# Holding back the first tile's value loads until the keys of the second and third head pair have landed

## The chip, the cores and the metric

The kernel runs on one core of a Trainium2 chip. A core has five engines that run their own instruction streams side by side: TensorE (PE in the profile, with its weight loads as PEld), VectorE (DVE), ScalarE (ACT), GpSimd (POOL) and SyncE (SP). Each engine works strictly through its own list, and waits at an instruction until what it needs is there. Transfers between DRAM and the on-chip memory SBUF are issued by SP, ACT or POOL and carried out by 16 DMA engines that all three share. The metric is the device time of one execution in microseconds (us); of several executions the median is given.

## What is computed

Two stages run one after the other. The first is attention in blocks of 64 tokens, for 8 batches, 8 heads, 576 tokens and a head size of 64:

```
q_c, k_c, v_c = (x.reshape(B, H, 9, 64, 64) for x in (q, k, v))
scores = 1/sqrt(64) * q_c @ k_c.T
attn   = exp(scores - max(scores)); attn = attn / (sum(attn) + 1e-9)
x      = (attn @ v_c) as tokens x (heads * 64)          # 4608 x 512
```

The second is a feed-forward layer on these 4608 rows, with weights 512 x 2048 and 2048 x 512:

```
h   = x @ w_in
g   = h where h >= 1;  0 where h <= -1;  (h + 1)^2 / 4 between
out = g @ w_out
```

All inputs are 4-byte floats, except that each weight comes as 8-byte words, two 32-bit halves of a number, from which the kernel first builds a high and a low part.

## The kernel before

**Tiles.** The 4608 tokens are cut into nine tiles of 512. In each tile the eight heads are taken as four pairs, called g = 0 to 3 here ("head groups" in the change's words). For each pair one tile of q, one of k and one of v is loaded, 128 x 512 floats (256 KB) each. The first tile (t = 0) has places of its own for most of these: the loads for pairs 2 and 3 go into memory in which the last weights will lie later, and are named after that place: `first_wi` in the trace is q and k of pairs 2 and 3, `first_wo` is v of these pairs and also some of the intermediate tiles of this stage. `q_sb`, `k_sb` and `v_sb` hold pairs 0 and 1.

**First tile's attention.** For one pair: TensorE turns q and k around (`flip`, L402), ACT copies the results out (L417), TensorE forms the scores (L435), DVE takes the maximum and subtracts it (L491, L507), ACT forms the exponentials (L510), DVE sums them and takes reciprocals (L516 to L518), POOL multiplies (L523), TensorE turns the result around and ACT copies it (L402, L537), TensorE multiplies by v (L457), and ACT and DVE split the result into a high and a low part (L562, L563). Only L457 needs v.

**Weights.** Each of the 32 weight blocks (wi0 to wi15, wo0 to wo15, 512 KB each) is loaded (L268, L275) and then prepared by three ACT and four DVE instructions (L290 to L319). The feed-forward products (L578 into the hidden layer, L612 out of it) of the first tile follow the weights as they become ready. From the second tile on they stay in SBUF, and attention of later tiles is woven between the products.

**Who sets the order.** Nothing is issued at once. Each step is handed to a `Plan` with the engine it runs on, a cost, what it reads and writes as names, and for loads a `lag` and a time for which the queue is `moving`. `Plan.emit` then plays these costs through and writes out each engine's instructions in the order of its due times. Of two steps that are both due when an engine comes free, the one added earlier goes first. Where TensorE would be idle by the plan, small filler products are put in (L1115, L1118). On the chip, the plan's times play no part any more: only the order within each engine is left, and the true dependences between tiles, on which instructions wait.

**First loads.** The list `first_loads` (L958) says which loads of the first tile go to which queue. q, k and the weights go to SP (k of pair 0 to ACT). The four v tiles go to POOL, in four transfers of 64 KB each (L377), with nothing that they wait for, so they are at the head of POOL's list. The q and k tiles go in two transfers of 128 KB each (L337). After them SP issues the loads of the second tile (L351, L367) and further weights.

Of the kernel before, what the change touches and what calls it, by code (L numbers as in the profile page):

```python
# [9 lines left out]
F32 = mybir.dt.float32  # L10
# [122 lines left out]
def kernel(  # L133
# [15 lines left out]
    nc = tc.nc  # L149
# [4 lines left out]
    P = 128  # L154
    C = 64
# [16 lines left out]
    def turn(t, g):  # L172
        if t <= ALONE:
            return t * NP + g
        d, m = divmod(t - ALONE - 1, 2)
        return (ALONE + 1) * NP + d * 2 * NP + 2 * g + m
# [3 lines left out]
    sb = ctx.enter_context(tc.tile_pool(name="sb", bufs=1))  # L180
    psum = ctx.enter_context(tc.tile_pool(name="psum", bufs=1, space=bass.MemoryType.PSUM))

    def buffers(pool, name, n, dtype=F32):
        return [
            (f"{name}{i}", pool.tile([P, T], dtype, name=f"{name}{i}")) for i in range(n)
        ]
# [3 lines left out]
    q_bufs, k_bufs, v_bufs = (buffers(sb, f"{n}_sb", 2) for n in "qkv")  # L190
# [50 lines left out]
    def room(name, bufs, t, g):  # L241
        if t == 0 and (name, g) in first:
            return first[name, g]
        if t > 0 and name in ("e", "x"):
            return wheel[(2 * turn(t, g) + (name == "x")) % 3]
        return bufs[turn(t, g) % len(bufs)]

    plan = Plan()
# [13 lines left out]
    def load_weight(w, j, queue="sp"):  # L262
        eng = queues[queue]

        def emit():
            words[w, j] = dst = place("words", w, j, [P, 2 * T], U32)
            if w == "wi":
                eng.dma_start(  # L268
                    out=dst.rearrange("p (kc f) -> p kc f", kc=KC),
                    in_=w_in[:, 2 * j * P:2 * (j + 1) * P].rearrange(  # L270
                        "(kc p) f -> p kc f", p=P
                    ),
                )
            else:
                eng.dma_start(out=dst, in_=w_out[j * P:(j + 1) * P, :])  # L275

        plan.add(queue, 0.65, emit, gate["ready"], (f"{w}{j}_0", f"{w}{j}_1"), lag=1.7, moving=1.4)
# [101 lines left out]
                    in_=rows.rearrange(split, r=2)[r],  # L379
                )  # L380

    def load_heads(t, g, which="qkv", queue="sp"):
        eng = queues[queue]

        for n, src, bufs in (("q", q, q_bufs), ("k", k, k_bufs), ("v", v, v_bufs)):
            if n not in which:
                continue
            key, dst = room(n, bufs, t, g)
            load = load_values if n == "v" else load_rows if t == 0 else load_blocks
            rows, parts = (1.4, 2) if load == load_rows else (1.4, 2 if t > 0 and BATCH[t] is not None else 4) if load == load_values else (  # L390
                (2.2, 4) if BATCH[t] is not None else (2.2, 8)
            )
            plan.add(
                queue, 0.65 * parts,
                lambda load=load, dst=dst, src=src: load(eng, dst, src, t, g),
                (), (key,), lag=1.7, moving=rows if queue == "sp" else 1.5 * rows,
            )

    def flip(ps, src):
# [553 lines left out]
    def load_next(n=1):  # L953
# [3 lines left out]

    first_loads = [  # L958
# [4 lines left out]
    ]  # L963
    for which, n, queue in first_loads:
        if which in ("wi", "wo"):
            load_weight(which, n, queue)
            loads.remove((which, n))
        else:
            load_heads(0, n, which, queue)

    for g in range(NP):
        attn_turn(0, g)
# [2 lines left out]
    for g in range(NP):  # L975
        attn_products(values_of(0, g))
        attn_split(0, g)

    load_heads(1, 0, "qk")
    load_next(2)  # L980
    load_heads(1, 0, "v")
    load_next(2)
    load_heads(1, 1)
# [66 lines left out]
    for t in range(ALONE + 1):  # L1050
        for j in range(NF):
# [4 lines left out]
            elif step in SPREAD:  # L1056
                n, m = SPREAD[step]
# [31 lines left out]
    for t in range(ALONE + 1, NTILE, 2):  # L1089
        units = [unit for p in range(NQ) for unit in whole(t, p)]  # L1090
        n = turn(t, 0) + 2 * NP
# [74 lines left out]
```

## Time and profile before

| | |
|---|---|
| time, median of 3 runs | 844.25 us (843.58 to 845.26) |
| the profiled execution | 845.72 us, of which the span on the page is 844.0 us |
| PE busy | 828.6 us (98% of the span) |
| DVE, ACT, POOL busy | 533.9, 469.1 and 272.0 us |
| DMA | 147.89 MB, mean 175 GB/s |
| packets by POOL's queue (q0) and by SP's (q1) | 30720 and 198368 |

The profile is of one execution. A page begins with busy times; the share of an engine over the whole span says little of one stage, so the start of the kernel is read here in views of short windows, in the timeline (each instruction with its start and length and, in brackets, the idle time before it and what ended it), and in the view of one tile's loads (how long an issue took, and how long it then was until the data had landed).

### The profile page before, as it was taken

How to read it: one execution, taken by the hardware profiler on the slowest of the kernel's cores; microseconds unless marked ns; L12 is line 12 of the kernel's file. 1: busy time of each engine (PE TensorE's matmuls, PEld its weight loads, DVE VectorE, ACT ScalarE, POOL GpSimd, SP SyncE). 2: the span in 40 equal slices, each digit the busy share in tenths (PEclk: the TensorE clock that was granted, in tenths of full speed). 3: DMA queues.
4: the chain of work that ended last, by engine and by line, in shares of the span. 5: the costliest groups of instructions: out<-in, count | busy, mean ns of one | idle time of the engine just before them, and what ended most of it. 6: DMA issues, size and time to landing. Idle time of an engine off the chain costs nothing.

```text
span 844.0 us, 16178 instructions
## 1 busy us (share of the span) xinstructions
PE 828.6 (98%) x5774; PEld 678.6 (80%) x5774; DVE 533.9 (63%) x941; ACT 469.1 (56%) x1001; POOL 272.0 (32%) x490
## 2 busy tenths in 40 slices
PE   6998999999999999999999999999999999999997
PEld 6786778888888888888888888888888888888886
DVE  3999997768788666756779427765593234343422
ACT  3889895555666645555566226555572255455422
POOL 5111110454434232343444114343432133333220
PEclk9999999999999999999999999999999999999999
DMA  9888732776878555977788418765545254444432
GB/s 218 231 254 232 227 65 58 205 220 177 217 173 240 102 135 142 260 214 212 205 209 245 157 58 243 215 192 183 173 155 183 62 189 171 153 147 164 152 98 75
DMA packets 230223, 147.89 MB, mean 175 GB/s; under 512 B 188672, under 2 KB 200448, under 8 KB 230144
## 3 DMA queue, kind: packets, MB, share of 16 engines
q0 software_dynamic: 30720, 89.68, 31.8%
q1 hardware_dynamic: 198368, 56.92, 29.2%
q8 instruction: 46, 0.75, 0.4%
q10 hardware_dynamic: 1056, 0.26, 0.2%
q14 instruction: 33, 0.27, 0.1%
HBM read 101.71 MB, written 36.70 MB: 164 GB/s over the span
## 4 chain that ended last, share of the span: by engine, by line
PE 92%; SPq 2%; DVE 2%; ACT 1%; DMA 1%; issue 1%; ACTq 0%; DVEq 0%
PE ps_o L612 45%; PE ps_h L828 27%; PE ps_h L578 15%; PE ps_a L457 2%; PE ps_a L435 2%; SPq L337 2%; DMA words_wi<-in_moe_w_in_dram 1%; PE ps_o L1115 0%; DVE tmp L626 0%; SPq L275 0%; ACT x L500 0%; ACT e L500 0%; SPq L268 0%; DVE tmp L305 0%; DVE tmp L300 0%
## 5 line engine op out<-in xcount | busy, mean ns | idle before, releaser
L612 PE MATMUL ps_o<-parts_wo,gh 128*128 128x512 f32 x1152 | 358.2, 392 | 0.4 <-DVE parts_wo L319 0.2
L612 PEld LDWEIGHTS ps_o<-parts_wo,gh 128*128 128x128 f32 x1152 | 214.6, 188 | 47.2 <-DVE tmp L626 1.5
L612 PE MATMUL ps_o<-parts_wo,gl 128*128 128x512 f32 x576 | 224.6, 390 | 0.0
L828 PE MATMUL ps_h<-x,ring 128*128 128x512 f32 x864 | 219.0, 389 | 0.0
L828 PEld LDWEIGHTS ps_h<-x,ring 128*128 128x128 f32 x864 | 162.2, 188 | 33.9
L599 DVE TENSOR_TENSOR gl<-r,gh 128x512 fp32r<-128x512 f32 x144 | 98.8, 687 | 105.9 <-ACT gh L597 105.0
L597 ACT CAST gh<-r 128x512 fp32r<-128x512 f32 x144 | 89.2, 621 | 129.1 <-PE ps_o L612 94.0
L808 POOL DMA_DIRECT2D ring<-combos x168 | 92.1, 549 | 168.1 <-PE ps_h L828 156.3
L578 PE MATMUL ps_h<-xh,parts_wi 128*128 128x512 f32 x384 | 131.3, 400 | 0.0
L612 PEld LDWEIGHTS ps_o<-parts_wo,gl 128*128 128x128 f32 x576 | 108.2, 188 | 22.9 <-DVE gl L599 0.2
L849 DVE TENSOR_TENSOR h<-ps_h,snaps 128x512 f32<-128x512 f32 x72 | 49.0, 680 | 76.6 <-ACT snaps L680 74.3
L578 PEld LDWEIGHTS ps_h<-xh,parts_wi 128*128 128x128 f32 x384 | 73.1, 190 | 16.3
L532 POOL DMA_DIRECT2D aT<-e x96 | 47.9, 505 | 118.7 <-issue 34.5
L859 DVE SCALAR_TENSOR_TENSOR r<-h,r 128x512 f32<-128x512 f32 x72 | 49.3, 685 | 58.0 <-ACT r L858 57.8
L680 ACT COPY snaps<-ps_h 128x512 f32<-128x512 f32 x72 | 42.1, 585 | 72.9 <-PE ps_h L828 72.2
L855 ACT ACTIVATE r<-h 128x512 f32<-128x512 f32 x72 | 45.5, 632 | 65.2 <-DVE h L849 63.7
L858 ACT ACTIVATE r<-r 128x512 f32<-128x512 f32 x96 | 60.5, 630 | 2.4
L933 POOL DMA_DIRECT2D r<-rest x48 | 26.2, 547 | 100.0 <-DVE gl L599 88.5
L578 PE MATMUL ps_h<-x_parts,parts_wi 128*128 128x512 f32 x128 | 50.7, 396 | 0.0
L897 POOL DMA_DIRECT2D rest<-r x48 | 26.2, 545 | 63.1 <-DVE r L859 62.1
L532 POOL DMA_DIRECT2D aT<-x x48 | 24.1, 506 | 65.1 <-DVE r L589 45.6
L585 ACT ACTIVATE r<-ps_h 128x512 f32<-128x512 f32 x48 | 29.2, 607 | 27.3 <-PE ps_h L578 27.1
(122 smaller groups left out, 969.1 us busy)
## 6 DMA issues: line engine op xcount, KB each, us to landing
ring<-combos POOLq DMA_DIRECT2D x168, 256.0 KB, 3.2
rest<-r POOLq DMA_DIRECT2D x48, 256.0 KB, 3.1
r<-rest POOLq DMA_DIRECT2D x48, 256.0 KB, 3.0
words_wi<-in_moe_w_in_dram SPq DMA_DIRECT2D x16, 512.0 KB, 8.2
words_wo<-in_moe_w_out_dram SPq DMA_DIRECT2D x16, 512.0 KB, 6.7
out_dram<-tmp SPq DMA_DIRECT2D x32, 256.0 KB, 3.8
combos<-tmp POOLq DMA_DIRECT2D x32, 256.0 KB, 3.6
q_sb<-in_q_dram SPq DMA_DIRECT2D x112, 64.0 KB, 3.8
```

What stands on the lines that cost most here:

```text
L532: queues[queue].dma_start(out=aT[b:b + Q, to], in_=x[a:a + Q, of])
L578: nc.tensor.matmul(out=ps, lhsT=weight["wi", j][:, half, kc * P:(kc + 1) * P], rhs=x, start=(kc == 0 and i == 0), stop=(kc == KC - 1 and i ...
L597: plan.add("act", 0.52, lambda: nc.scalar.copy(out=gh, in_=now(r)), (rkey,), (ghkey,), ahead=ahead)
L599: plan.add("dve", 0.6, lambda: nc.vector.tensor_tensor(out=gl, in0=now(r), in1=gh.bitcast(F32), op=ALU.subtract), (rkey, ghkey), (glkey,), ...
L612: nc.tensor.matmul(out=acc, lhsT=x[:, cols], rhs=weight["wo", j][:, half, :], start=(j == 0 and i == 0), stop=(j == NF - 1 and i == 2),)
L680: "act", cost, lambda: nc.scalar.copy(out=out(), in_=src()), reads, writes, ahead=ahead
L808: plan.add("pool", 0.55, lambda: nc.gpsimd.dma_start(out=ap().bitcast(F32), in_=combos[d][:, n, :].bitcast(F32)), (f"dram{d}_{n}",), (key, ...
L828: nc.tensor.matmul(out=ps, lhsT=w()[:, at:at + P], rhs=y(), start=name in FRESH and i == 0 and k == 0, stop=i == 1 and k == 2, skip_group_ ...
L849: plan.add("dve", 0.62, lambda: nc.vector.tensor_tensor(out=o(), in0=source[1](), in1=ap(), op=ALU.add), (source[0], skey), (okey,), ahead ...
L855: plan.add("act", 0.52, lambda: nc.scalar.activation(out=now(r), in_=h(), func=AF.Relu, bias=0.5, scale=0.5), (hkey,), (rkey,), ahead=50)
L858: plan.add("act", 0.52, lambda: nc.scalar.square(out=now(r), in_=now(r)), (), (rkey,), ahead=50)
L859: plan.add("dve", 0.6, lambda: nc.vector.scalar_tensor_tensor(out=now(r), in0=h(), scalar=1.0, in1=now(r), op0=ALU.max, op1=ALU.min), (hke ...
```

## The change

The first tile's v loads get something to wait for. A tile `latch` of 128 x 16 floats (64 bytes in each of the 128 partitions) is added in SBUF. `await_k(n)` adds a POOL instruction that copies one column of k of pair n into one column of `latch`; it can run only when that k has landed. The v loads of pairs 0 and 1 are put behind `await_k(1)`, those of pairs 2 and 3 behind `await_k(2)`. That the loads read `latch` is said to the plan only: on the chip they come later because POOL works through its list in order. In `first_loads` the first v is moved behind q and k of pair 2, so that these keys are known by name when they are needed; the order on SP's queue stays.

```
-    def load_heads(t, g, which="qkv", queue="sp"):
+    def load_heads(t, g, which="qkv", queue="sp", needs=()):
...
                 lambda load=load, dst=dst, src=src: load(eng, dst, src, t, g),
-                (), (key,), lag=1.7, moving=rows if queue == "sp" else 1.5 * rows,
+                needs, (key,), lag=1.7, moving=rows if queue == "sp" else 1.5 * rows,
...
-        ("wi", 1, "sp"), ("v", 0, "pool"), ("q", 2, "sp"), ("k", 2, "sp"), ("v", 1, "pool"),
+        ("wi", 1, "sp"), ("q", 2, "sp"), ("k", 2, "sp"), ("v", 0, "pool"), ("v", 1, "pool"),
...
+    latch = sb.tile([P, C // 4], F32, name="latch")
+
+    def await_k(n):
+        key, src = room("k", k_bufs, 0, n)
+        plan.add("pool", 0.1, lambda: nc.gpsimd.tensor_copy(out=latch[:, :1], in_=src[:, :1]), (key,), ("latch",))
+
     for which, n, queue in first_loads:
         if which in ("wi", "wo"):
             load_weight(which, n, queue)
             loads.remove((which, n))
-        else:
-            load_heads(0, n, which, queue)
+            continue
+        if which == "v" and n in (0, 2):
+            await_k(1 + n // 2)
+        load_heads(0, n, which, queue, ("latch",) if which == "v" else ())
```

## The prediction

> **What bounds the kernel now.** I read the chain of work that ended last first, then the busy times by window, then the first 37 us instruction by instruction. The columns of the windows are busy time of PE, PEld, DVE, ACT and POOL, granted TensorE clock, DMA share and GB/s.
>
> ```profile
> PE 92%; SPq 2%; DVE 2%; ACT 1%; DMA 1%; issue 1%; ACTq 0%; DVEq 0%
> ```
> ```profile
> 10.00:35.00 25.00, 20.05 (x331) 16.99 (x325) 19.32 (x37) 17.35 (x32) 8.01 (x10) 1.00 0.96 234
> 35.00:115.00 80.00, 77.30 (x563) 61.85 (x563) 78.83 (x151) 69.08 (x174) 16.19 (x32) 0.96 0.82 223
> 115.00:840.00 725.00, 724.47 (x4846) 593.24 (x4844) 434.59 (x753) 379.70 (x794) 240.70 (x432) 1.00 0.58 168
> ```
>
> From 115 us on PE is busy 724.47 of 725 us: nothing at the start can change that stretch, only move it. From 35 to 115 us DVE is busy 78.83 of 80 us: it builds the weights' parts, and PE, with fillers counted as busy, has more slack than DVE. So the time at which PE's solid stretch begins is set by how early DVE gets into its own solid stretch. Before it, from 10 to 35 us, DVE works only 19.32 of 25 us: 5.68 us of idle time is what an earlier start can win. Where does it lie?
>
> ```profile
> 10.25 0.49 DVE L293 TENSOR_SCALAR tmp<-tmp 128x512 uint32<-128x512 uint32 x1 [8.85 <-ACT tmp L290]
> ...
> 11.85 0.68 DVE L507 TENSOR_TENSOR e<-ps_a,mx 128x512 f32<-128x512 f32 x1
> ...
> 14.31 0.66 PE L402 MATMUL ps_o<-ident,k_sb 128*128 128x128 f32 x4 [1.79 <-DMA k_sb<-in_k_dram]
> ...
> 15.01 0.58 ACT L417 COPY first_wo<-ps_o 128x512 f32<-128x512 f32 x1 [2.53 <-PE ps_o L402]
> 15.49 0.63 ACT L510 ACTIVATE e<-e 128x512 f32<-128x512 f32 x1
> ...
> 16.15 0.69 DVE L516 TENSOR_REDUCE sm<-e 128x8 f32<-128x512 f32 x1 [3.02 <-ACT e L510]
> ...
> 21.80 0.69 DVE L516 TENSOR_REDUCE sm<-e 128x8 f32<-128x512 f32 x1 [1.02 <-ACT e L510]
> ...
> 30.94 0.69 DVE L516 TENSOR_REDUCE sm<-first_wo 128x8 f32<-128x512 f32 x1 [0.72 <-ACT first_wo L510]
> ```
>
> The reader is to follow the 3.02 us backwards. DVE waits for the first pair's exponentials on ACT (15.49); they could have run when DVE's subtraction (11.85) ended at 12.5, but ACT stood in its list at the copy of the second pair's turned keys (15.01, idle 2.53); that waited for TensorE's turn at 14.31, and this for the load of k of pair 1. One late load holds PE, ACT and DVE, and it is the load that the first latch names. The other two DVE waits (1.02, 0.72) again end with exponentials that stand behind other things in ACT's list.
>
> ```profile
> L337 SPq DMA_DIRECT2D k_sb<-in_k_dram x1: 1932/1932/1932, 5.5 to 5.5; - x1
> ...
> DMA to landing us min/median/max: 8.7/8.7/8.7
> ```
>
> Issued at 5.5 us and 8.7 us under way, it landed at 14.2. What it shared the DMA engines with until then is in the view of the queues, first from 1 to 14.2 us, then from 9 to 12 and from 17 to 20 us (packets, MB, share of 16 engines):
>
> ```profile
> q1 hardware_dynamic: 4648, 1.92, 70.4%
> q0 software_dynamic: 341, 0.72, 26.0%
> q10 hardware_dynamic: 1056, 0.26, 10.6%
> ```
> ```profile
> q1 hardware_dynamic: 1113, 0.29, 64.0%
> q0 software_dynamic: 169, 0.34, 56.0%
> ```
> ```profile
> q1 hardware_dynamic: 1148, 0.74, 101.5%
> q0 software_dynamic: 15, 0.02, 2.5%
> ```
>
> q1 is SP's queue, q10 ACT's, q0 POOL's, which so early carries v alone. With v beside it SP's queue got 64% of the engines (9 to 12 us); with v gone, 101.5%. And v is in no hurry:
>
> ```profile
> 0.35 0.10 POOL L1149 MEMSET const-uint8-127<- 128x1 uint8 x1
> ...
> 1.46 5.04 POOL L377 DMA_DIRECT2D v_sb<-in_v_dram  x8 [0.15 <-issue]
> ...
> 17.44 1.04 POOL L523 TENSOR_TENSOR e<-e,sm 128x512 f32<-128x512 f32 x1 [3.22 <-DVE sm L518]
> 23.07 1.31 POOL L523 TENSOR_TENSOR e<-e,sm 128x512 f32<-128x512 f32 x1 [4.59 <-DVE sm L518]
> 28.61 1.04 POOL L523 TENSOR_TENSOR first_wo<-first_wo,sm 128x512 f32<-128x512 f32 x1 [4.23 <-DVE sm L518]
> ```
> ```profile
> 25.90 0.65 PE L457 MATMUL ps_a<-aT,v_sb 64*64 64x64 f32 x32
> 29.13 0.69 PE L457 MATMUL ps_o<-aT,v_sb 64*64 64x64 f32 x32
> ...
> 32.41 0.69 PE L457 MATMUL ps_a<-first_wi,first_wo 64*64 64x64 f32 x32 [0.86 <-ACT first_wi L537]
> ...
> 35.73 0.69 PE L457 MATMUL ps_o<-first_wi,first_wo 64*64 64x64 f32 x32
> ```
>
> The four pairs' values are first used at 25.90, 29.13, 32.41 and 35.73.
>
> **The change, part by part.** *What goes from the front.* Until k of pair 1 lands, q0 takes 26.0% of 13.2 us, that is 3.4 us of all engines. If SP's queue would be served no faster without it, the gain is 0; if it gets all of that time, 3.4 us. The shares add up to 107%, so packets overlap and not all of it comes back: 3.4 / 1.07 = 3.2. The jump from 64% to 101.5% lies near the upper end, but the first loads are held by issue and start-up too. I take 2.6 us: k lands at about 11.6.
>
> The Trainium skill (DMA: Bandwidth & Descriptors, Queues, rings and completion order) says that each DMA engine takes its queues in turn, packet by packet. The 64% beside 56% agrees; by that rule alone the term would be the whole 3.2 us, and the sum 0.6 us lower.
>
> *What the earlier k is worth.* TensorE's turn, ACT's copy, the exponentials and DVE's sum all stand directly behind it, so 2.6 of the 3.02 us go. DVE's 5.68 us of idle time cap the whole. The 1.02 us wait hangs on ACT's list behind the same chain; I count nothing for it, since pair 2's q and k now share the engines with v of pairs 0 and 1. I take 0.2 us off for what DVE meets later: 2.4 us.
>
> *What v costs in its new place.* The first latch comes free at about 11.7. The copy itself (one column) is not in the trace; the nearest rows are POOL's memset of one column at the start, 0.10 us, and its 1.04 us for 512 columns; I take 0.1, and either end falls into POOL's idle time. Then eight issues follow. An issue of v took 5.04 / 8 = 0.63 us, so POOL is in them until 16.7. Behind them in POOL's list stands pair 0's multiply, at 17.44 today: covered. If k landed at 13, POOL would be free at 18.1, the multiply 0.7 late; its result was used at 25.90, which hides that as well.
>
> *The second latch.* The plan lets it read k of pair 2, and lets it write `latch` only when the loads that read it have landed. By the plan's constants (2.6 for each v's issue, 2.1 for moving, 1.7 and 0.15 behind) and with k of pair 1 due at 10.0 and 0.25 for the first latch, that is at 10.25 + 2.6 + 2.6 + 2.1 + 1.85 = 19.4, after the multiplies of pairs 0 and 1 and before that of pair 2. This fixes POOL's order: latch, v of 0 and 1, two multiplies, latch, v of 2 and 3, two multiplies. What is queued behind the second latch is thus eight issues and the multiply of pair 2, at 28.61 today, for which PE's turn, ACT's copy and L457 of pair 2 wait. With pair 1's multiply 2.4 us earlier (23.07 + 1.31 - 2.4 = 22.0), v of pair 2 is issued until 24.5 and v of pair 3 until 27.0. Pair 2's multiply, due at 28.61 - 2.4 = 26.2, is then up to 0.8 us late. How long such a v load takes from issue to landing:
>
> ```profile
> v_sb<-in_v_dram POOLq DMA_DIRECT2D x8, 64.0 KB, 7.0
> first_wo<-in_v_dram POOLq DMA_DIRECT2D x8, 64.0 KB, 6.9
> ```
>
> At 6.9 us from the end of the issue at the worst, v of pair 2 is there by 31.4, v of pair 3 by 33.9. They are wanted at 32.41 - 2.4 = 30.0 and 35.73 - 2.4 = 33.3. That is the tight place: counted from the start of an issue it is 30.8 and 33.3, and in a queue less crowded than that of the first 14 us it is less (k of the second tile, below, took 3.0). I take it as just hidden, and what it costs where it is not as up to 1.4 us of the 2.4, which is the lower bound of the gain in the forecast.
>
> *What moves on SP's queue.* Nothing in its order. All bytes up to 33 us are the same, so the second tile's q and k land at about the same time:
>
> ```profile
> 27.43 3.06 SPq L351 DMA_DIRECT2D k_sb<-in_k_dram  x3
> ```
> ```profile
> k_sb<-in_k_dram SPq DMA_DIRECT2D x4, 64.0 KB, 3.0
> ```
> ```profile
> 36.46 0.70 DVE L411 STREAM_TRANSPOSE kT<-k_sb 128x512 f32<-128x512 f32 x1
> ```
>
> The last k there is issued at about 30 and lands at 33; DVE reads it at 36.46, so 3.5 us of shift are covered, and 2.4 fit.
>
> **The sum.** 2.6 - 0.2 = 2.4 us. Against the profiled execution (845.72 us, of which 844.0 are the span) that makes 843.3; its median neighbours lie at 844.25, so I forecast 841.9. The added tile shifts later tiles by 64 bytes, for which I count nothing: no row shows a cost of an address.
>
> **Rivals.** *The swap is even* (0.22). v leaves the front, but its 1 MB must pass before 36 us anyway; if pair 2's k, the weights and v of pair 2 arrive as late as now, ACT's list ends with the same wait. For it speaks the tight place above: 2.4 - 1.4 leaves 1.0, and another wait in ACT's list takes the rest. Against it, that behind 21.80 the longest wait of DVE up to 35 us is the 0.72 shown, so that ACT and DVE have other work in hand there. Time 843.2 to 844.3.
>
> *A wait for v takes the place of the wait for k: slower* (0.13). The second latch stands behind pair 1's multiply. If that does not move forward, v of pair 2 is issued from 24.38 to 26.8 and lands at 33.7, against 32.41 wanted: 1.3 us lost, and PE, which idles 0.86 there now, idles over 2 us. This decides at about 23.0: a second latch that opens later makes PE wait longer than today. What a wait of such a length does to the clock:
>
> ```profile
> 80.97 1.33 PE L457 MATMUL ps_a<-aT,v_sb 64*64 64x64 f32 x32 [2.36 <-ACT e L500]
> ```
> ```profile
> 80.00:90.00 10.00, 9.03 (x55) 7.34 (x56) 9.52 (x20) 8.60 (x22) 3.98 (x8) 0.66 1.07 350
> ```
>
> After 2.36 us of idle PE the granted clock was 0.66 over 10 us, 3.4 us lost. So 845.6 without that and 849.0 with it; I take 847.
>
> The Trainium skill (SBUF — State Buffer, Who interferes with whom) says that a DVE instruction in a two-port mode shuts GpSimd out of writing the descriptors of its own DMAs, and v would now be issued while DVE is busy. That speaks for this rival. The trace does not bear it out so far:
>
> ```profile
> 49.95 3.98 POOL L532 DMA_DIRECT2D aT<-e  x8 [16.69 <-DVE gl L599]
> ```
>
> These eight issues took 0.50 us each at a time when DVE hardly paused.
>
> *More than the forecast* (0.07): the full 3.2 us and the 1.02 us wait as well, 840.0.
>
> *The change doesn't hold v back* (0.02): POOL runs its list in order, so only if the copy were not to wait. Time 844.25.
>
> **How the numbers follow.** The forecast (841.9; by its bounds of 1.0 to 3.4 us, 840.8 to 843.2) has 0.56. A measurement of this kernel can tell about 0.2%, 1.7 us, from no change, so below 842.6 counts as faster: 0.47 of the forecast and the 0.07, 0.54 in all. Within it lie 0.09 of the forecast, 0.22 and 0.02: 0.33. Slower is 0.13. The range leaves out the tail of the slow rival and that of the largest gain: 839.8 to 845.6.
>
> **What would show it.** Right: k of pair 1 turned near 11.7 instead of 14.31; DVE's wait of 3.02 under 1 us; POOL's 16 issues of L377 in two bursts, near 12 to 17 and 20 to 27; L457 of pair 0 near 23.5; DVE's first L411 before 33; the rest of the trace shifted by one amount. Wrong: L457 of pair 2 or 3 waiting for `first_wo` from DRAM; a lower clock between 25 and 40 us; DVE idle between 30 and 60; or an earlier start that is gone by 115 us, which would mean that PE, ACT or the weights' loads bound that stretch and not DVE.

## The result, and the profile after

| | time, us | runs |
|---|---|---|
| before | 844.06 (843.58 to 845.26) | 4 |
| after | 855.66 (855.33 to 855.97) | 4 |
| ratio after / before | 1.0135, interval 1.0118 to 1.0153 | |

The change makes the kernel 11.6 us slower. (Ratios here are of the runs' means; times are medians.) The profiled execution took 855.97 us, its span 854.2 us.

The first view is the page of the changed kernel: span, busy times, the chain of work that ended last, and the largest groups of products. Lines of the code behind the change stand up to 8 higher in number; L968 is the copy of the latch. L828, in all kernels, forms the hidden layer from the fourth tile on: the rows (`x`) are streamed past combinations of weights that are read back from DRAM into `ring`.

```profile
span 854.2 us, 16186 instructions
...
PE 840.2 (98%) x5774; PEld 678.1 (79%) x5774; DVE 535.0 (63%) x941; ACT 470.7 (55%) x1001; POOL 273.3 (32%) x492
...
PE 88%; SPq 4%; DMA 3%; DVE 3%; ACT 1%; issue 1%; DVEq 0%; ACTq 0%
...
L612 PE MATMUL ps_o<-parts_wo,gh 128*128 128x512 f32 x1152 | 362.1, 395 | 2.5 <-DVE parts_wo L319 2.5
...
L612 PE MATMUL ps_o<-parts_wo,gl 128*128 128x512 f32 x576 | 226.5, 393 | 0.0
L828 PE MATMUL ps_h<-x,ring 128*128 128x512 f32 x864 | 223.4, 395 | 0.0
```

PE is busy 840.2 us, 11.6 more than the 828.6 of before, while the largest wait among its great groups is 2.5 us: no wait has come in that is worth 11.6 us. So look first whether the predicted start took place. The timeline of the changed kernel, in the same stretch as that of before:

```profile
10.36 0.43 POOL L968 COPY latch<-k_sb 128x1 f32<-128x1 f32 x1 [9.05 <-DMA k_sb<-in_k_dram]
...
10.56 0.60 PE L402 MATMUL ps_o<-ident,k_sb 128*128 128x128 f32 x4
...
10.79 5.05 POOL L377 DMA_DIRECT2D v_sb<-in_v_dram  x8
...
12.35 0.69 DVE L516 TENSOR_REDUCE sm<-e 128x8 f32<-128x512 f32 x1 [0.40 <-ACT e L510]
...
20.47 0.38 POOL L968 COPY latch<-first_wi 128x1 f32<-128x1 f32 x1
...
20.79 4.90 POOL L377 DMA_DIRECT2D first_wo<-in_v_dram  x8
...
23.64 0.69 PE L457 MATMUL ps_a<-aT,v_sb 64*64 64x64 f32 x32
...
31.59 0.69 PE L457 MATMUL ps_a<-first_wi,first_wo 64*64 64x64 f32 x32
...
31.83 0.70 DVE L411 STREAM_TRANSPOSE qT<-q_sb 128x512 f32<-128x512 f32 x1
...
34.55 0.66 ACT L290 ACTIVATE tmp<-words_wo 128x512 f32<-128x512 f32 x1 [3.16 <-DMA words_wo<-in_moe_w_out_dram]
...
35.73 0.69 PE L457 MATMUL ps_o<-first_wi,first_wo 64*64 64x64 f32 x32 [1.94 <-ACT first_wi L537]
```

It did, and rather more than predicted: the latch opens at 10.36, k of pair 1 is turned at 10.56 instead of 14.31, DVE's wait of 3.02 is 0.40, v is issued in two bursts, and DVE begins the second tile's q 3.4 us earlier (31.83 against 35.26). No product waits for a v load. Up to here the start is better, and yet the kernel ends later, so something behind it costs.

Now the windows. Two rows of the changed kernel, and then two of before (busy time of PE, PEld, DVE, ACT, POOL with instructions, granted clock, DMA share, GB/s):

```profile
140.00:854.00 714.00, 709.90 (x4676) 573.52 (x4674) 412.65 (x712) 363.32 (x759) 241.38 (x432) 1.00 0.59 170
...
700.00:800.00 100.00, 100.00 (x431) 80.96 (x430) 39.65 (x59) 50.20 (x85) 30.08 (x55) 1.00 0.42 147
```
```profile
140.00:844.00 704.00, 699.47 (x4679) 573.02 (x4677) 412.12 (x713) 363.50 (x763) 240.70 (x432) 1.00 0.59 173
...
700.00:800.00 100.00, 99.96 (x441) 82.35 (x440) 40.99 (x61) 51.04 (x86) 30.11 (x56) 1.00 0.44 158
```

At 140 us both kernels have nearly the same work left, 4676 and 4679 products. The changed one needs 714 us for it and the other 704; PE is idle for 4.1 and 4.5 us of that, most of it at the very end, and the clock is granted in full. Between 700 and 800 us every product has 512 columns: 441 of them fit into 100 us before, 431 after. That is 226.8 and 232.0 ns each. **Not a wait, but each product is some 5 ns longer** in this stretch.

That can be read off a few lines. The timeline of the changed kernel and that of before, PE alone (start, duration, and how many instructions a line merges):

```profile
761.74 1.56 PE L828 MATMUL ps_h<-x,ring 128*128 128x512 f32 x6
763.14 0.63 PE L612 MATMUL ps_o<-parts_wo,gh 128*128 128x512 f32 x2
```
```profile
763.66 1.52 PE L828 MATMUL ps_h<-x,ring 128*128 128x512 f32 x6
765.02 0.61 PE L612 MATMUL ps_o<-parts_wo,gh 128*128 128x512 f32 x2
```

Six products take 763.14 - 761.74 = 1.40 us after and 765.02 - 763.66 = 1.36 us before, 233 and 227 ns each. The mean of a group's durations hides this, 395 ns in the page above against 392 in the page of before:

```profile
L612 PE MATMUL ps_o<-parts_wo,gh 128*128 128x512 f32 x1152 | 358.2, 392 | 0.4 <-DVE parts_wo L319 0.2
```

That is so since the products are pipelined and overlap; the distance from start to start is the measure.

### The profile page after: what moved, and what is told of

It is laid out like the page before. It is cut to its first block, busy times and chain, and to the rows that moved or that the text cites. A ratio compares the mean times of both kernels' runs of the same rounds, so it can differ in the third digit from the quotient of the medians.

```text
span 854.2 us, 16186 instructions
## 1 busy us (share of the span) xinstructions
PE 840.2 (98%) x5774; PEld 678.1 (79%) x5774; DVE 535.0 (63%) x941; ACT 470.7 (55%) x1001; POOL 273.3 (32%) x492
## 4 chain that ended last, share of the span: by engine, by line
PE 88%; SPq 4%; DMA 3%; DVE 3%; ACT 1%; issue 1%; DVEq 0%; ACTq 0%
PE ps_o L612 44%; PE ps_h L828 27%; PE ps_h L578 13%; PE ps_a L457 2%; PE ps_a L435 2%; SPq L351 2%; DMA words_wo<-in_moe_w_out_dram 1%; SPq L337 1%; DMA k_sb<-in_k_dram 1%; SPq L268 1%; DMA q_sb<-in_q_dram 1%; DVE tmp L305 1%; DMA words_wi<-in_moe_w_in_dram 1%; DVE tmp L300 0%; DVE r L589 0%
## 5 line engine op out<-in xcount | busy, mean ns | idle before, releaser
L612 PE MATMUL ps_o<-parts_wo,gh 128*128 128x512 f32 x1152 | 362.1, 395 | 2.5 <-DVE parts_wo L319 2.5
L612 PEld LDWEIGHTS ps_o<-parts_wo,gh 128*128 128x128 f32 x1152 | 214.8, 188 | 54.2 <-DVE parts_wo L319 3.9
L612 PE MATMUL ps_o<-parts_wo,gl 128*128 128x512 f32 x576 | 226.5, 393 | 0.0
L828 PE MATMUL ps_h<-x,ring 128*128 128x512 f32 x864 | 223.4, 395 | 0.0
L828 PEld LDWEIGHTS ps_h<-x,ring 128*128 128x128 f32 x864 | 162.6, 188 | 37.2
L578 PE MATMUL ps_h<-xh,parts_wi 128*128 128x512 f32 x384 | 131.2, 400 | 0.0
L612 PEld LDWEIGHTS ps_o<-parts_wo,gl 128*128 128x128 f32 x576 | 108.2, 188 | 24.5 <-DVE gl L599 0.4
L578 PEld LDWEIGHTS ps_h<-xh,parts_wi 128*128 128x128 f32 x384 | 72.1, 188 | 17.3
L578 PE MATMUL ps_h<-x_parts,parts_wi 128*128 128x512 f32 x128 | 50.5, 394 | 0.1
```

Of the source, the lines that this page charges most:

```text
L578: nc.tensor.matmul(out=ps, lhsT=weight["wi", j][:, half, kc * P:(kc + 1) * P], rhs=x, start=(kc == 0 and i == 0), stop=(kc == KC - 1 and i ...
L612: nc.tensor.matmul(out=acc, lhsT=x[:, cols], rhs=weight["wo", j][:, half, :], start=(j == 0 and i == 0), stop=(j == NF - 1 and i == 2),)
L828: nc.tensor.matmul(out=ps, lhsT=w()[:, at:at + P], rhs=y(), start=name in FRESH and i == 0 and k == 0, stop=i == 1 and k == 2, skip_group_ ...
```

## The experiments

What could lengthen a product far from the change? The change alters no code of the later stages. But `Plan` plays the new waits through and writes another order: in the two traces the lists of all five engines differ in places up to 265 us; behind that each engine's list is the same in both, and the products between 700 and 800 us are longer all the same. What is altered besides is where tiles lie. In the built programs `latch` takes 64 bytes of each partition, and 24 weight blocks (wi0 to wi11, wo0 to wo11), with the places of later tiles' x that reuse them, lie behind it. Before, they begin at multiples of 256 bytes; after, 64 bytes past one. The last four blocks of each kind, `xh`, `xl`, `gh` and `gl` stay where they were. **Theory A:** an operand of TensorE that doesn't begin at a multiple of 256 bytes costs some ns per product. **Rival B:** the new order of the loads and of the engines' lists, or the copies on POOL, disturb something later. **Rival C:** any shift, whatever its size, costs.

### The tile alone, and its size

The kernel before with nothing but the tile:

```
+    latch = sb.tile([P, C // 4], F32, name="latch")
```

> The kernel before with only the 64-byte tile added, without the copies, the waits or the changed order. It moves the 24 weight blocks that are placed after it by 64 bytes and does nothing else. Address theory (products are slower when operands start 64 bytes off a 128-byte line): 855 to 857 us, about 12 us over the kernel before, and 512-column products that follow each other at about 231 ns instead of 227. Order theory (the new order and waits make the products slower): 844 us, 227 ns.

The changed kernel with `latch` of 128, 256 and 32 bytes:

```
-    latch = sb.tile([P, C // 4], F32, name="latch")
+    latch = sb.tile([P, C // 2], F32, name="latch")     # 128 bytes; [P, C]: 256; [P, C // 8]: 32
```

> The changed kernel with a latch of 128 bytes instead of 64, so that the weight blocks start at a multiple of 128 again, but not of 256. Address theory with a step of 128 bytes: 841.5 to 842.5 us, the gain of about 2 us of the earlier start without the loss. Address theory with a step of 256 bytes: still about 855. Order theory: 855.7 us, as the changed kernel.

> The changed kernel with a latch of 256 bytes, so that the weight blocks start at multiples of 256 as in the kernel before. Address theory, whatever its step up to 256: 841.5 to 842.5 us. Order theory: 855.7 us.

> The changed kernel with a latch of 32 bytes: the 24 weight blocks behind it start 32 bytes past a multiple of 256. If any start off a multiple of 256 costs about the same, as 64 and 128 bytes did: 855 to 857 us, 512-column products 231 to 233 ns apart. If the loss follows how far into the 256 bytes a row starts: between 842 and 855 us.

| kernel | shift, bytes | time, us | before beside it | ratio, interval |
|---|---|---|---|---|
| before + tile alone | 64 | 855.64 | 843.97 | 1.0141 (1.0127 to 1.0154) |
| the change, 32-byte tile | 32 | 860.11 | 844.05 | 1.0189 (1.0175 to 1.0203) |
| the change as it is | 64 | 855.66 | 844.06 | 1.0135 (1.0118 to 1.0153) |
| the change, 128-byte tile | 128 | 856.35 | 843.97 | 1.0150 (1.0136 to 1.0164) |
| the change, 256-byte tile | 256 | **842.21** | 843.97 | 0.9985 (0.9976 to 0.9994) |

An unused tile of 64 bytes, with no copy, no wait, no load moved and every engine's list as in the kernel before, costs 11.7 us: the whole loss comes without rival B. A shift of 256 bytes costs nothing, so it isn't any shift (C). The 32-byte tile costs more than the expectation had for any case (855 to 857 us). That the changed kernel (855.66) is no faster than the tile alone (855.64) suggests that its better start gained nothing by the end; the part on the prediction comes back to that. The window from 700 to 800 us, of the kernel with the tile alone, then of the change with 256 bytes, then with 32:

```profile
700.00:800.00 100.00, 100.00 (x430) 80.95 (x430) 39.63 (x59) 50.08 (x85) 30.05 (x55) 1.00 0.42 143
```
```profile
700.00:800.00 100.00, 99.95 (x441) 82.35 (x440) 40.31 (x60) 49.33 (x83) 29.86 (x55) 1.00 0.47 155
```
```profile
700.00:800.00 100.00, 100.00 (x431) 80.47 (x430) 38.79 (x58) 50.38 (x85) 29.93 (x55) 1.00 0.44 145
```

441 products again with 256 bytes, 430 and 431 with 64 and 32. With 256 bytes the change is no longer slower, and by the medians it is the fastest kernel of the study: 842.21 us, 1.8 below the runs of before beside it by medians, 0.5 to 2.0 by the interval of the ratio.

### Which operands pay

If it is the address of TensorE's operands, then a shift of tiles that TensorE never reads should be free, and the tiles that it reads should pay one by one. In the kernel before, with pairs of unused tiles that move some tiles to 64 past a multiple of 256 and bring the next back to a multiple:

```
+    sb.tile([P, 16], F32, name="pad0")      # 64 bytes
...
+    sb.tile([P, 48], F32, name="pad1")      # 192 bytes
```

Moved are `x_parts`, `xh`, `xl`, `r`, `gh`, `gl` and `tmp` together; `r` and `tmp` alone, which ACT, DVE and POOL use and TensorE does not; `gh` and `gl` alone, which L612 loads into the array while `parts_wo` is streamed past them; `x_parts`, `xh` and `xl` alone, which are streamed in L578 and for a part in L828.

> The kernel before, with 64 bytes put in front of the activations (x_parts, xh, xl, r, gh, gl, tmp) and 192 behind them, so that these start 64 bytes past a multiple of 256 and all weight blocks at a multiple of 256. L578 then streams shifted columns against weights loaded from aligned ones; L612 the other way round. If the streamed operand pays: L578 at 231 ns or more, L612 at 227, in all some 2 us (384 + 128 + 64 products of L578, and those of L828 that read xl). If the loaded weights pay: L612 at 231, L578 at 227, some 7 us (1728 products at 4 ns). If both pay: both slower, 9 us or more.

> The kernel before with only r and tmp 64 bytes past a multiple of 256 (64 bytes in front of each, 192 behind). ACT, DVE and transfers use these tiles, TensorE never reads them. If only TensorE's own reads matter: 844 us, 227 ns. If accesses of other engines to tiles off 256 bytes also slow the products beside them (the products of aligned operands that came slower in the two shifted kernels, wo12 to wo15 there and L828 here): 846 us or more, with 228 ns or more.

> The kernel before with only gh and gl 64 bytes past a multiple of 256. They are loaded as weights for L612 alone, 1728 products. If the loaded operand pays by itself: L612 at 231 to 233 ns, 7 to 11 us (1728 x 4 to 6 ns), 851 to 855 us; L578 and L828 at 227. If only the streamed operand pays: 844 us.

> The kernel before with only x_parts, xh and xl 64 bytes past a multiple of 256. TensorE streams them in L578 (576 products) and in those products of L828 that read xl (144). If the streamed operand pays by itself: these at 231 ns or more, some 3 us (720 x 4 ns), 846 to 848 us; L612 at 227. If only the loaded operand pays: 844 us.

The last of this group asks whether still more alignment pays: the change with 256 bytes, and 128 bytes more before `ident` and before `x_parts`, so that q, k, v, `qT`, `kT`, `e` and `aT`, which lie 128 past a multiple of 256 in the kernel before, begin at multiples of 256 as well.

> The changed kernel with the 256-byte latch, and 128 bytes more in front of the identity tile and of x_parts: the attention tiles q, k, v, qT, kT, e, aT and x, 128 bytes past a multiple of 256 until now, then start at multiples of 256 like all others. If the 64-row products of L435 and L457 pay for their offset as the large ones do (4 to 6 ns for each of 1072): up to 4 us less than with the 256-byte latch, 838 to 841 us. If such small pieces don't pay, or ready products are not what their stage waits for: 842.2 us.

| moved to 64 past 256 | time, us | before beside it | ratio, interval |
|---|---|---|---|
| all seven | 858.87 | 844.05 | 1.0179 (1.0164 to 1.0195) |
| `r`, `tmp` | 843.83 | 843.79 | 1.0001 (0.9992 to 1.0011) |
| `gh`, `gl` | 857.18 | 843.79 | 1.0162 (1.0147 to 1.0177) |
| `x_parts`, `xh`, `xl` | 848.98 | 843.79 | 1.0065 (1.0048 to 1.0082) |
| (none: everything at a multiple of 256, with the change) | 842.67 | 844.11 | 0.9994 (0.9977 to 1.0011) |

The window from 700 to 800 us, with `r` and `tmp` moved, then with `gh` and `gl`:

```profile
700.00:800.00 100.00, 99.96 (x441) 82.34 (x440) 40.34 (x60) 50.38 (x85) 30.17 (x55) 1.00 0.46 155
```
```profile
700.00:800.00 100.00, 100.00 (x435) 81.39 (x434) 39.93 (x60) 50.27 (x86) 30.15 (x55) 1.00 0.44 145
```

Moving the tiles that only the other engines use costs nothing here; moving either kind of TensorE's operands does. The next table gives the mean distance between the starts of successive products in ns, worked out from the trace's start times of all pairs within one column that begin after 50 us and lie 200 to 300 ns apart (`wo0 to 11` and so on: the weight blocks that the products read, by their order in the built program):

| kernel | L612, wo0 to 11 | L612, wo12 to 15 | L578, wi0 to 11 | L578, wi12 to 15 | L828 |
|---|---|---|---|---|---|
| before | 227.1 | 227.0 | 227.7 | 227.6 | 226.7 |
| after | 230.3 | 229.3 | 233.2 | 229.9 | 231.6 |
| tile alone, 64 bytes | 230.3 | 229.1 | 233.1 | 229.6 | 231.5 |
| `gh`, `gl` moved | 233.4 | 233.5 | 229.3 | 229.3 | 229.1 |
| `x_parts`, `xh`, `xl` moved | 228.4 | 228.2 | 230.2 | 230.2 | 228.8 |

The sum comes near. L612 runs 1152 + 576 = 1728 times, three quarters of them with wo0 to wo11; L578 576 times; L828 1008 times (counts of the trace's groups). For the tile alone: 1296 x 3.2 + 432 x 2.1 + 432 x 5.4 + 144 x 2.0 + 1008 x 4.8 ns = 4.1 + 0.9 + 2.3 + 0.3 + 4.8 = 12.4 us, against 11.7 measured. For `gh` and `gl`, L612 alone gives 1728 x 6.4 ns = 11.1 of the 13.4 us between the medians; with 576 x 1.6 ns of L578 and 1008 x 2.4 ns of L828, whose operands were not moved, it is 14.4, one more than measured.

What this leaves open: products whose own operands are all aligned become slower as well, when others are shifted; the expectations had these at 227. L612 with wo12 to wo15 goes from 227.0 to 229.3 in the changed kernel, and L828 to 229.1 where only `gh` and `gl` moved. Where `x_parts`, `xh` and `xl` moved, L578, which streams them, became 2.5 ns longer, and L612, which reads none of them, 1.2 to 1.3. So how much of the cost belongs to a product's own operands, and how much is spread over others, is not separated; and all seven moved together cost 14.8 us, less than the 13.4 and 5.2 of two of its parts. It isn't merely the neighbour: with `gh` and `gl` moved, L828 products that follow one another are 229.1 ns apart, and those followed by an L612 226.8. I found no reason, and no run here looks for one. Nor is it shown what in TensorE's reading makes 256 bytes the unit; the runs show only that 32, 64 and 128 cost and 256 doesn't. And keeping q, k, v and the small tiles at multiples of 256 too brought nothing that could be measured: its interval, 0.9977 to 1.0011, holds both no change and the whole gain of the 256-byte latch, and single runs went from 841.38 to 849.80. (The expectation counts 1072 products of L435 and L457; in the trace they are 1152 each, so a cost of 4 to 6 ns on every one would have been 9 to 14 us, had it gone into the time in full.)

### What the start is worth

With the address out of the way, the forecast's own chain can be tested. Against the change with 256 bytes, the first copy reads another tile, and all else, the order on each engine included, is kept: `ident`, which is there from the start, so that v of pairs 0 and 1 waits for nothing; or k of pair 0, which lands earlier than k of pair 1.

```
         key, src = room("k", k_bufs, 0, n)
+        if n == 1:
+            src = ident            # in the other kernel: room("k", k_bufs, 0, 0)[1]
```

> The changed kernel with the 256-byte latch and the same order on every engine, but the first copy reads the identity tile, which is there from the start: v of pairs 0 and 1 is issued at 1.5 us again, v of pairs 2 and 3 as in the changed kernel. If the gain comes from k of pair 1 landing earlier because v of pairs 0 and 1 is out of its way: k of pair 1 is turned at 13 to 14 us instead of 10.6 and most of the gain is lost, 843.3 to 844 us. If it comes from the other order or from v of pairs 2 and 3 alone: 842.2 us as with the 256-byte latch.

> As the one before, but the first copy waits for k of pair 0, which lands at about 6.5 us, 4 us ahead of k of pair 1. If the gain goes with how much v is out of the way of k of pair 1: in between, k of pair 1 turned at 11.5 to 12.5 us, 842.5 to 843.5 us. If DVE's start is not what sets the end: the same time as the others of the 256-byte latch, 842.2 us, whenever k is turned.

And the kernel before, unchanged, for a second profile:

> The kernel before, unchanged, for a second profile: in the first the granted clock was 0.5 for 6.8 us from 80.6 us on. If that is part of every run of this kernel, the gain of the 256-byte latch (1.8 us in the medians) comes in part from its absence there; if the second profile has no such stretch, the span is 841.5 to 842.5 us and the gain is the earlier start alone.

| kernel | k of pair 1 turned | DVE's first L411 | time, us | before beside it | ratio, interval |
|---|---|---|---|---|---|
| before | 14.31 | 35.26 | | | |
| before again | 13.36 | 34.41 | 843.76 | 843.79 | 1.0001 (0.9991 to 1.0012) |
| 256 bytes, first copy on `ident` | 13.01 | 32.07 | 843.56 | 844.05 | 0.9990 (0.9981 to 0.9999) |
| 256 bytes, first copy on k of pair 0 | 10.03 | 32.51 | 844.72 | 844.05 | 1.0011 (1.0001 to 1.0021) |
| 256 bytes, as the change has it | 9.78 | 30.53 | 842.21 | 843.97 | 0.9985 (0.9976 to 0.9994) |

The two profiles of the kernel before differ by 0.95 us in the first column and 0.85 in the second, so less than that says nothing here.

By the medians the wait on k of pair 1 is worth about 1.4 us (842.21 against 843.56). But each was run beside its own runs of before, and the intervals against these overlap (0.9976 to 0.9994 and 0.9981 to 0.9999): that the wait on k is what pays is not shown. The kernel whose first copy waits for nothing is faster than before by its own interval. It shares with the 256-byte kernel the second latch and the new order on all engines, and its windows show DVE as far on at 115 us (the 256-byte kernel's are below):

```profile
10.00:35.00 25.00, 21.09 (x339) 18.21 (x340) 21.41 (x41) 17.47 (x33) 9.88 (x13) 1.00 1.04 271
35.00:115.00 80.00, 77.14 (x536) 60.56 (x537) 79.48 (x153) 72.09 (x178) 15.82 (x32) 1.00 0.77 212
```

That is 41 + 153 = 194 instructions, the same as with the full change. How much of the gain belongs to the new order and how much to the loads held back, the runs don't separate.

The kernel with k of pair 0 should have landed between the two, and did not: k of pair 1 was turned at 10.03, nearly as early as with the full change, yet it is the slowest. Its timeline suggests why (the profiled execution is its slowest, 846.83 us). PE's turns of pair 2 and ACT's work on the weights, first of this kernel, then of the change with 256 bytes:

```profile
17.51 0.63 PE L402 MATMUL ps_o<-ident,first_wi 128*128 128x128 f32 x4 [2.25 <-DMA first_wi<-in_k_dram]
...
34.89 0.66 ACT L290 ACTIVATE tmp<-words_wo 128x512 f32<-128x512 f32 x1 [3.52 <-DMA words_wo<-in_moe_w_out_dram]
```
```profile
14.00 0.60 PE L402 MATMUL ps_o<-ident,first_wi 128*128 128x128 f32 x4
...
31.51 0.67 ACT L290 ACTIVATE tmp<-words_wo 128x512 f32<-128x512 f32 x1 [1.63 <-DMA words_wo<-in_moe_w_out_dram]
```

With v let go at 6.27 us instead of 9.95, k of pair 2 comes 3.5 us later (17.51 against 14.00) and a block of weights 3.4 (34.89 against 31.51). So the first k is likely not the only load that matters: k of pair 2 and the weights are in the same race. The windows of these two kernels, in the same order:

```profile
10.00:35.00 25.00, 20.75 (x298) 17.88 (x296) 19.41 (x38) 15.11 (x29) 10.99 (x16) 0.93 0.95 233
35.00:115.00 80.00, 76.11 (x554) 59.69 (x555) 76.70 (x147) 70.96 (x176) 15.80 (x32) 0.98 0.81 224
```
```profile
10.00:35.00 25.00, 21.35 (x335) 18.05 (x334) 21.81 (x41) 18.41 (x34) 14.88 (x22) 1.00 1.09 269
35.00:115.00 80.00, 77.16 (x536) 60.35 (x535) 79.41 (x153) 71.08 (x175) 15.81 (x32) 1.00 0.77 211
```

DVE does 38 + 147 = 185 instructions from 10 to 115 us in the first and 41 + 153 = 194 in the second. In the profiled execution of the kernel with k of pair 0 the granted clock was also below 1 (0.93 and 0.98).

## Why the prediction was wrong

**The step that failed** is one sentence of the sum: "The added tile shifts later tiles by 64 bytes, for which I count nothing: no row shows a cost of an address." The cost was 11.7 us (the tile alone), over six times the 1.8 us that the change gained with a 256-byte tile. For the copy, which the trace doesn't show either, the prediction took bounds from the nearest rows; for the address no row could give one, since all operands of the 512-column products lay at multiples of 256, and a term with an open end was put at nothing. None of the rivals had it either: the one on the slower side was a wait for v, and no L457 waited for v. The Trainium skill (SBUF — State Buffer, Operand start alignment) asks only that an operand start at a multiple of its element's size, and says that this is about legality and that its runs timed nothing; 64 bytes is legal by it, and these runs show what it costs.

**What bounds the kernel** was read rightly, with a consequence that was missed. PE is without idle time from 115 us on; so nothing at the start can change that stretch, the prediction says, "only move it". But in such a stretch a cost on each product goes into the time in full: some 2% of 227 ns on 3312 products is worth more than the wait of 3.02 us that the change was after.

**k of pair 1: right, a little small.** It was to land 2.6 us earlier, at most 3.4. It was turned at 10.56 in the changed kernel and at 9.78 with 256 bytes, against 14.31 and 13.36 in the two profiles of before: 2.8 to 4.5 us earlier, about 3.7 between the middles (10.17 and 13.83). So 2.6 was low by about 1 us, and three of the four differences are above the upper bound of 3.4. It counted the time that v's packets took, with SP's work up to k taken as fixed. The view of the queues of the changed kernel, from 1 to 10.3 us:

```profile
q1 hardware_dynamic: 4124, 1.73, 85.2%
q10 hardware_dynamic: 1056, 0.26, 13.8%
```

SP's queue had moved 1.73 MB when k was there, against 1.92 MB before, in 0.852 x 9.3 = 7.9 us of all engines against 0.704 x 13.2 = 9.3. Without v in the way less of SP's later loads had passed before the last of k; by these two profiles these 1.4 us would come on top of q0's 3.4 in the bound.

**The signs named for the start: right.** DVE's wait of 3.02 became 0.40. POOL's two bursts came at 10.79 to 15.84 and 20.79 to 25.69 (said: 12 to 17, 20 to 27), the first L457 at 23.64 (said: 23.5), the first L411 at 31.83 (said: before 33). The copies took 0.43 and 0.38 us rather than 0.1; POOL had the room.

**v of pairs 2 and 3: right that they are in time.** The tight place held; L457 of pair 2 ran at 31.59 without a wait. But that of pair 3 ran at 35.73, the very time of before, where the sum wanted 33.3. PE's 1.94 us before it came from ACT, which stood 3.16 us before a block of `words_wo`.

**What DVE meets later: put at 0.2 us, and it was more.** Two new waits came in behind the one that went. The first is the chain of k of pair 1 once more, with k of pair 3: TensorE's turn, ACT's copy of it, the exponentials of pair 2 behind that copy, DVE's sum. The second stands behind ACT's 3.16 us for `words_wo`:

```profile
22.48 0.63 PE L402 MATMUL ps_o<-ident,first_wi 128*128 128x128 f32 x4 [1.20 <-DMA first_wi<-in_k_dram]
23.14 0.59 ACT L417 COPY first_wi<-ps_o 128x512 f32<-128x512 f32 x1 [1.59 <-PE ps_o L402]
24.10 0.64 ACT L510 ACTIVATE first_wo<-first_wo 128x512 f32<-128x512 f32 x1
24.84 0.69 DVE L516 TENSOR_REDUCE sm<-first_wo 128x8 f32<-128x512 f32 x1 [2.24 <-ACT first_wo L510]
...
36.20 0.69 DVE L563 TENSOR_TENSOR x_parts<-ps_a,xh 128x512 fp32r<-128x512 f32 x1 [2.16 <-ACT xh L562]
```

The windows of the changed kernel say what was left of the lead:

```profile
10.00:35.00 25.00, 19.96 (x303) 16.86 (x301) 20.89 (x39) 15.89 (x29) 15.38 (x22) 1.00 0.98 242
35.00:115.00 80.00, 76.78 (x559) 59.61 (x560) 77.94 (x149) 71.86 (x178) 15.86 (x32) 1.00 0.80 221
```

DVE has done 39 + 149 = 188 instructions between 10 and 115 us, as many as before (37 + 151), where the 256-byte kernel has done 194. (The second profile of before has 37 + 154 = 191.) Apart from the address, this looks like the rival "the swap is even": other loads came late instead, and ACT's list passed their waits on. The 256-byte kernel has the same lists and kept its lead; why its loads came earlier is not shown.

**"Nothing in its order": wrong behind the first loads.** In the traces SP's list is the same up to about 31 us; then v of the second tile goes ahead of two weight blocks, and between 64 and 93 us the weight loads come in another order, as the plan wrote it.

**Carried one to one: wrong.** In the changed kernel none of the lead reaches the end, as the 188 instructions and the times of it and of the tile alone say. With the 256-byte tile DVE starts its second tile 3.9 to 4.7 us earlier (30.53 against 34.41 and 35.26), and 1.8 us of that reach the end. The prediction had named the sign: "an earlier start that is gone by 115 us, which would mean that PE, ACT or the weights' loads bound that stretch". The chain of waits of the 256-byte kernel goes through weights and second-tile loads from 50 to 88 us. These are its longest pieces there, with start and duration:

```profile
53.34 5.07 DMA q_sb<-in_q_dram
...
64.32 4.25 DMA words_wo<-in_moe_w_out_dram
...
73.06 7.39 DMA words_wo<-in_moe_w_out_dram
...
84.58 3.47 DMA k_sb<-in_k_dram
```

Nearly the same bytes have to pass by then in both orders, which fits loads that bound this stretch beside DVE. That the loads ate the difference is argued from this chain, not shown by a run.

Also a part of the comparison with before: the first profile of the kernel before has its granted clock at 0.5 for 6.8 us from 80.6 us on, at the end of the wait of 2.36 us that the prediction quotes, and the 256-byte kernel's has not. The second profile of before, in its window there:

```profile
80.00:90.00 10.00, 9.84 (x63) 7.87 (x64) 9.96 (x20) 9.24 (x19) 4.00 (x8) 0.83 0.82 224
```

0.83 over 10 us is 1.7 us lost, against 3.4 in the first profile, and the spans of the two differ by 844.0 - 842.2 = 1.8. So some of the 1.8 us gained may be a wait that is gone, and a clock with it, rather than work done earlier; the runs don't separate the two.

## What to carry to other kernels

A small tile that is put into SBUF moves all that is allotted behind it. Before you cost such a tile at nothing, look at the start addresses of TensorE's operands, and make the tile as wide as keeps them at multiples of 256 bytes: here, with a tile of 256 bytes instead of 64, +11.6 us became -1.8.

Where an engine is without idle time for 85% of a kernel, read the distance between its instructions before and after, not their waits, and not the mean duration of pipelined ones: a window that counts instructions in 100 us showed it at once (441 and 431).

A load that is held back gains for what is in front of it, and what the bytes cost later belongs to the same sum; the load that first waits isn't the only one in the race. And where a planner writes the order, a new dependence moves more than the steps that it names: compare the lists of all engines before you put a gain down to one wait.

## What the runs showed of the hardware

Products of 128 x 512 in this kernel follow one another at about 227 ns if their operands begin at multiples of 256 bytes in each partition. With operands 64 bytes past that they were 2.5 to 6.4 ns longer in the cases above, in both roles: 6.4 ns in L612 where the loaded operand was moved (`gh` and `gl`), 2.5 ns in L578 where the streamed one was. Products that read no moved tile were up to 2.4 ns longer in the same kernels. The smallest shift cost most: 16.1 us for 32 bytes, 11.6 for 64, 12.4 for 128, each against the runs of before beside it and with the gain of the start inside. Where `r` and `tmp`, which only ACT, DVE and POOL use, were moved by 64 bytes, the ratio was 1.0001 (0.9992 to 1.0011).

The Trainium skill (DMA: Bandwidth & Descriptors, Queues, rings and completion order) says that each DMA engine takes its queues in turn, packet by packet. The 64% beside 56% agreed as shares of the engines' time; in the packets that the same view counts, 1113 beside 169, no even turn shows. What the removal of one queue was worth to k, about 3.7 us between the middles of two profiles each, is near the 3.2 us that the prediction drew from that rule, and nearer than the 2.6 that it took.
